# Turning a sixth pair of second-layer weights in the plain part of a retention and two-layer feed-forward kernel

## The chip, the cores and the metric

The kernel runs on one core of one Trainium2 chip. The metric is device time in microseconds (us) of that core; 831.47 us is the median of three runs before the change (830.78 to 833.61). In what follows PE is the matrix engine, PEld its weight loads, DVE the vector engine, ACT the scalar engine, POOL the GpSimd engine and SP the engine that issues most transfers.

## The reference

Retention over 4 batches, 8 heads, 576 positions and a head width of 64, then two feed-forward layers over the 2304 tokens, each 512 to 2048 to 512, all in fp32:

```python
scores = scale * np.matmul(q, k.transpose(0, 1, 3, 2))
ret = scores * Dmat[None, :, :, :]          # decay gamma**(i-j), causal
attn_out = np.matmul(ret, v)
...
h = x @ w_in;  g = np.maximum(h, 0.0) + alpha * np.minimum(h, 0.0);  x = g @ w_out     # layer 1
h = x @ w_in;  g = h * (1.0 / (1.0 + np.exp(-1.702 * h)));           x = g @ w_out     # layer 2
```

## The kernel before

**Stages.** The retention of 16 head pairs runs first, as loop iterations 0 to 16. Then comes the *plain part*: layer 1 on 1536 of the 2304 tokens, in three chunks of 512 tokens, 48 steps. A step is one hidden block of 128 rows: 12 products of `mm1` (h from x and `wi`) and 12 of `mm2` (acc from g and `wo`), the second two steps later. Chunk 0 and 1 use the blocks in pieces (`BLOCKS`); hidden blocks 0 and 1 are used in steps 0 to 3 and then not before step 32, when chunk 2 begins. Then come four *rounds* of 768 tokens. Round 0 is the rest of layer 1, rounds 1 to 3 are layer 2. A round is a two by two block product with seven products in place of eight (Strassen's scheme with sums of blocks), 112 units of 6 products each: units 0 to 55 make the hidden layer (`unit1`), units 56 to 111 the output (`unit2`). Every operand of a product is split into two rounded parts, `hi` and `lo`: ACT copies, DVE subtracts.

**Turning weights.** The weights come as raw 8-byte words, 16 rows of 128 x 1024 for each layer. A row is loaded in two halves of 0.5 MB (`w_piece`), gets three passes on ACT (`w_sat`, `w_range`, `w_top`: L129, L133, L137) and one on DVE (`w_low`, L144). Two rows make a *pair*, and `pair2` plans a pair of layer 2: eight sums of quarters (`p_sums`, L174), a store of the plain quarters to DRAM (`r_store`, tensor `rg`), the `hi` copies on ACT (`b_hi`) and `lo` subtractions on DVE (`b_lo`, L192), and a store of the finished blocks (`b_store`, tensors `sm` and `sp`). Rounds 1 to 3 read these back: `r_load` and `r_split` for the first product of a round, `s_load` (tiles `ws`) for the second. In round 0 the second product reads the layer 1 blocks that `p_store` and `plain_store` wrote.

**What sets the order.** Every engine runs its own program in order. The order is written by hand: `at(time, fn, ...)` puts a piece of work at a time, counted in iterations, in half steps of the plain part (`half(n)`) or in units of the rounds, and `run_to` emits what is due. Loads of `pair2` are issued by POOL's queue in the plain part and by SP's in the rounds; a transfer that must wait for its tile holds up what stands behind it in the same queue. Tiles share places by tag: `w0` holds the first-layer weights `wi[0]` of hidden blocks 0 and 1, `w8` their second-layer weights `wo[0]`, and `cv`, `raw1`, `w1`, `X1` to `X4` take rows in turn.

**Before**, pairs 0 to 4 of layer 2 are turned in the plain part, pair 5 straddles its end and the first half of round 0, pair 6 is turned in round 0 (units 43 to 113) and pair 7 in round 1 (units 117 to 156). In round 0, POOL makes the 16 differences of hidden blocks that the second product needs (`g_sum`), and the two of each hidden pair that `after1` calls `t1` and `t2`. In iteration 4 of the retention ACT's program has the first pass over row 0 of the layer 1 weights (`layer1`, m = 0).

Of the kernel before, what the change touches and what calls it, by code (L numbers as in the profile page):

```python
# [46 lines left out]
def kernel(  # L47
# [11 lines left out]
    nc = tc.nc  # L59
# [28 lines left out]
    r1 = [dram.tile([128, 2, 4, 256], F32, name=f"r1_{j}") for j in range(NJ)]  # L88
    sp = [[dram.tile([128, 3, 4, 2, 256], F32, name=f"sp{n}_{h}") for h in range(2)] for n in (1, 2)]
# [149 lines left out]

    def row(key, src, home, load, when, eng):  # L240
        at(load[0], w_load, key, src, home)
        for c, t in enumerate(load):
            at(t, w_piece, key, src, c, eng)
        for t, fn in zip(when, (w_sat, w_range, w_top, w_low)):
            at(t, fn, key)

    def pair2(j, t, homes, load, rows, sums, store, hi, lo, late, eng):
        for e in range(2):
            row((2, 2 * j + e), w2, homes[e], [t(n) for n in load[e]] if type(load[e]) is tuple else (t(load[e]),) * 2, [t(n) for n in rows[e]], eng)
        for g in range(2):  # L250
            at(t(sums[g]), p_sums, 2, j, g, nc.gpsimd if j > 3 else nc.vector)
        at(t(store), r_store, j)
        for n in range(2):
            at(t(hi[n]), b_hi, j, n)
            at(t(lo[n]), b_lo, j, n)
        at(t(late), b_store, j)
# [381 lines left out]
    def s_load(r, n):  # L638
        i, h = divmod(n, 2)
        t = ws["s", n] = slot(RING[n % (5 if r else 3)], [128, 4, 2, 256], F32R, "ws2")  # L640
        l = min(r, 1)
        src = sm[l][h][:, SUM[i]] if i in SUM else sp[l][h][:, i // 3]
        nc.sync.dma_start(out=t.bitcast(F32), in_=src)
# [172 lines left out]
    for m, home, load, when, hi, lo in (  # L816
        (0, "cv", (2.8, 3.8), (4.75, 5.75, 6.75, 8.0), 8.25, 9.0),
# [40 lines left out]
    for j, n in enumerate((12, 20, 26, 28, 48, 50, 53, 60)):  # L858
        at(half(n), plain_store, j)
    for j, plan in enumerate((  # L860
# [16 lines left out]
    with tc.manual_schedule():  # L877
# [74 lines left out]
        for k in range(NK):  # L952
            at(base + (26.0, 26.4, 29.9, 30.4)[k], x_load, 2, k)
            at(base + (29.7, 30.1, 30.8, 31.2)[k], x_split, 2, k, xp[1])
        for c, home, t in ((1, "X3", 27), (0, "X1", 32)):
            at(base + t, part_load, c, home)
        for k in range(2):
# [5 lines left out]
            5, lambda u: 1e3 + u, ("raw1", "X2"), (3.7, 9),  # L963
            ((22.1, 22.2, 24.1, 25.3), (29.1, 29.2, 31.1, 32.3)), (33, 33.1), 38.6, (43.1, 43.2), (44.3, 45.4), 46.5,
            nc.sync,
        )
# [21 lines left out]
        for j, homes, *plan in (  # L988
# [4 lines left out]
        ):  # L993
            pair2(j, float, homes, *plan, nc.sync)
        for r in range(R):
# [34 lines left out]
            for j in range(8):  # L1030
                at(z + 7.3 + 2.4 * j, g_sum, 0, 4, 0, j, None if r else nc.gpsimd)
                at(z + 25.6 + 2.4 * j, g_sum, 3, 3, 4, j, None if r else nc.gpsimd)
# [82 lines left out]
```

## Time and profile before

| | before |
|---|---|
| median of three runs | 831.47 us |
| the profiled execution: its time, its span | 831.47 us, 829.8 us |
| PE busy | 806.6 us (97%) |
| PEld busy | 745.2 us (90%) |
| DVE busy | 649.4 us (78%) |
| ACT busy | 531.1 us (64%) |
| POOL busy | 124.6 us (15%) |
| moved by DMA | 210.67 MB, 254 GB/s |
| mean granted PE clock | 0.991 |

The span runs from the first to the last instruction; the run's time has 1.7 us more around it. A busy engine is one with an instruction in work; the profile counts products as pipelined, so PE's share says little, and its gaps and the length of a stage say more.

### The profile page before, as it was taken

What the parts mean: (1) busy time and instruction counts of PE and PEld (TensorE: products, weight loads), DVE (VectorE), ACT (ScalarE), POOL (GpSimd) and SP (SyncE); (2) the same over time, 40 slices, a digit from 0 to 9 for tenths busy, and PEclk for the clock granted to TensorE, in tenths of its full rate; (3) what the DMA queues carried; (4) which work ended last, traced back from release to release, by engine and by line L of the source; (5) the groups of instructions that cost most, each with busy time, mean ns of one, the idle gap of its engine ahead of it and who ended that gap; (6) DMA issues with size and microseconds to landing.
All of it is one profiled execution on the core that took longest, in us unless ns stands there. A gap on an engine that the chain in (4) does not pass through costs nothing.

```text
span 829.8 us, 14143 instructions
## 1 busy us (share of the span) xinstructions
PE 806.6 (97%) x5004; PEld 745.2 (90%) x5004; DVE 649.4 (78%) x1157; ACT 531.1 (64%) x961; POOL 124.6 (15%) x134
## 2 busy tenths in 40 slices
PE   9899999999999999899998989999999999999998
PEld 8798888888888888789797989999999999999998
DVE  7587987886475677768999868989777799777875
ACT  7579969775354865454774677766566667566653
POOL 2231111100002106326647003000000000000000
PEclk9999999999999999999998999999999999999999
DMA  9896999635878673986977684988443986445881
GB/s 348 352 359 225 347 368 365 247 147 216 316 245 305 215 264 103 321 312 223 355 276 257 228 270 135 362 316 313 137 134 99 363 308 215 148 130 197 293 270 72
DMA packets 87053, 210.67 MB, mean 254 GB/s; under 512 B 7875, under 2 KB 43715, under 8 KB 78534
## 3 DMA queue, kind: packets, MB, share of 16 engines
q1 hardware_dynamic: 81072, 188.78, 64.1%
q0 software_dynamic: 5760, 20.97, 7.4%
q8 instruction: 39, 0.64, 0.3%
q14 instruction: 32, 0.26, 0.1%
q10 hardware_dynamic: 150, 0.02, 0.0%
HBM read 150.50 MB, written 59.24 MB: 253 GB/s over the span
## 4 chain that ended last, share of the span: by engine, by line
PE 77%; DMA 6%; DVE 5%; issue 3%; ACT 2%; POOL 2%; SPq 1%; POOLq 0%; ACTq 0%; DVEq 0%
PE acc L654 24%; PE h L654 18%; PE h L479 15%; PE acc L520 14%; PE av L318 3%; DMA rg<-raw 1%; POOL raw L174 1%; DMA ws<-r 1%; PE sc L318 1%; PE st L318 1%; DMA raw<-in_w_dram 1%; DVE tm L174 1%; DMA x<-os 1%; DMA ws<-sp 1%; DVE gsf L104 1%
## 5 line engine op out<-in xcount | busy, mean ns | idle before, releaser
L104 DVE TENSOR_TENSOR gsf<-g,gsf 128x384 fp32r<-128x384 f32 (+1 forms) x272 | 169.8, 638 | 39.2 <-ACT gsf L99 38.3
L99 ACT ACTIVATE gsf<-g 128x384 fp32r<-128x384 f32 (+1 forms) x272 | 145.6, 542 | 76.5 <-PE acc L654 32.4
L654 PE MATMUL acc<-gsf,ws 128*128 128x384 f32 x768 | 136.5, 335 | 2.4 <-DVE gsf L104 1.5
L479 PE MATMUL h<-x,wi 128*128 128x512 f32 x576 | 138.2, 389 | 0.0
L520 PE MATMUL acc<-gsf,wo 128*128 128x512 f32 x576 | 138.2, 389 | 0.0
L654 PEld LDWEIGHTS acc<-gsf,ws 128*128 128x128 f32 x768 | 133.3, 188 | 4.2 <-DVE gsf L104 2.9
L654 PE MATMUL acc<-x,ws 128*128 128x384 f32 x660 | 129.9, 337 | 4.1 <-ACT tm L99 4.1
L520 PEld LDWEIGHTS acc<-gsf,wo 128*128 128x128 f32 x576 | 108.0, 188 | 22.8 <-ACT raw L99 0.4
L479 PEld LDWEIGHTS h<-x,wi 128*128 128x128 f32 x576 | 108.0, 188 | 22.5
L654 PEld LDWEIGHTS acc<-x,ws 128*128 128x128 f32 x660 | 116.1, 189 | 6.0 <-ACT tm L99 6.0
L654 PE MATMUL h<-x,ws 128*128 128x384 f32 x540 | 109.1, 337 | 3.8 <-DVE g L487 1.9
L654 PE MATMUL h<-gsf,ws 128*128 128x384 f32 x576 | 106.6, 341 | 3.4 <-DVE gsf L104 3.4
L654 PEld LDWEIGHTS h<-gsf,ws 128*128 128x128 f32 x576 | 101.8, 192 | 6.2 <-DVE gsf L104 6.2
L654 PEld LDWEIGHTS h<-x,ws 128*128 128x128 f32 x540 | 95.4, 189 | 4.7 <-issue 2.2
L487 DVE SCALAR_TENSOR_TENSOR g<-g,rise_sb,h 128x512 f32<-128x512 f32 (+1 forms) x49 | 36.4, 743 | 52.2 <-ACT g L492 52.0
L174 DVE TENSOR_TENSOR tm<-h,tm 128x384 f32<-128x384 f32 x97 | 53.5, 552 | 26.3 <-PE h L654 22.5
L492 ACT ACTIVATE g<-h 128x512 f32<-128x512 f32 (+1 forms) x49 | 29.1, 594 | 54.7 <-PE h L479 54.7
L174 DVE TENSOR_TENSOR g<-g 128x384 f32<-128x384 f32 x96 | 54.0, 563 | 0.7
L99 ACT ACTIVATE tm<-acc 128x384 f32<-128x384 f32 x62 | 30.3, 488 | 37.7 <-PE acc L654 34.2
L125 POOL DMA_DIRECT2D raw<-in_w_dram x40 | 21.1, 533 | 196.4 <-ACT raw L137 44.2
L104 DVE TENSOR_TENSOR ws<-pad,ws 128x512 fp32r<-128x512 f32 x66 | 39.7, 622 | 9.2 <-ACT ws L99 9.2
L174 POOL TENSOR_TENSOR g<-g 128x384 f32<-128x384 f32 x32 | 40.4, 1280 | 40.0 <-DVE g L487 38.5
(101 smaller groups left out, 979.7 us busy)
## 6 DMA issues: line engine op xcount, KB each, us to landing
ws<-sm SPq DMA_DIRECT2D x32, 1024.0 KB, 6.5
ws<-sp SPq DMA_DIRECT2D x24, 1024.0 KB, 5.6
raw<-in_w_dram POOLq DMA_DIRECT2D x40, 512.0 KB, 7.7
sm<-raw SPq DMA_DIRECT2D x32, 512.0 KB, 4.7
raw<-in_w_dram SPq DMA_DIRECT2D x24, 512.0 KB, 7.8
pad<-rg SPq DMA_DIRECT2D x48, 256.0 KB, 2.8
ld<-in_qkv_dram SPq DMA_DIRECT2D x13, 864.0 KB, 7.5
r<-raw SPq DMA_DIRECT2D x16, 512.0 KB, 3.1
```

What stands on the lines that cost most here:

```text
L99: return nc.scalar.activation(out=out, in_=in_, func=ACTF.Copy)
L104: latest[0] = eng.tensor_tensor(out=out, in0=a, in1=b.bitcast(F32), op=ALU.subtract)
L125: eng.dma_start(out=raws[key][:, c * DM:c * DM + DM], in_=f[:, c * DM:c * DM + DM])
L174: latest[0] = (eng or nc.vector).tensor_tensor(out=out, in0=x, in1=y, op=op)
L318: return nc.tensor.matmul(out=out, lhsT=lhsT, rhs=rhs, start=start, stop=stop, skip_group_check=True)
L479: nc.tensor.matmul(out=t, lhsT=w[:, cw, k * 128:k * 128 + 128], rhs=x[:, cx], start=(i == 0), stop=(i == 3 * NK - 1),)
L487: nc.vector.scalar_tensor_tensor(out=g[0], in0=g[1], scalar=rise_sb[:, m:m + 1], in1=h, op0=ALU.mult, op1=ALU.add)
L492: nc.scalar.activation(out=out, in_=in_, func=ACTF.Relu, scale=-1.0)
L520: nc.tensor.matmul(out=acc[0][d], lhsT=w[:, d // 2, cw, d % 2 * 128:d % 2 * 128 + 128], rhs=g[:, cx], start=(m == m0 and i == 0), stop=(m ...
L654: nc.tensor.matmul(out=out, lhsT=w(cw), rhs=x(cx), start=(start and n == 0), stop=True, skip_group_check=True,)
```

## The change

One more pair of layer 2 is turned in the plain part. Places `w0` and `w8` are lent to it: `wi[0]` and half of `wo[0]` are written to DRAM at the end of the retention (`evict`; the rest of `wo[0]` lies there anyway, since `plain_store(0)` moves ahead), pair 0 is turned in their place in steps 14 to 27, and they are read back on POOL's queue in steps 29.5 and 31 (`bring_wi`, `bring_wo`), before step 32 uses them. The old pairs 0 to 4 become 1 to 5, pair 6 takes the straddling plan of the old pair 5, and pair 7 has its loads and ACT passes in the second half of round 0 and the rest in the first half of round 1. `g_sum` of round 0 goes from POOL to DVE, and so do the sums of pair 7; other stores, the x splits of chunk 2 and the place of a partial sum move; the first passes over row 0 of layer 1 move from iterations 4 to 6 of the retention to 6 to 7.

```diff
+    def evict(j):
+        nc.sync.dma_start(out=kept[j // 2][0], in_=wi[j].bitcast(F32))
+        nc.sync.dma_start(out=kept[j // 2][1], in_=wo[j].bitcast(F32)[:, 1, 0])
+
+    def bring_wi(j):
+        wi[j] = wp.tile([128, 2, 2, DM], F32R, tag=f"w{HOME[j]}", name="wi")
+        nc.gpsimd.dma_start(out=wi[j].bitcast(F32), in_=kept[j // 2][0])
+
+    def bring_wo(j):
+        wo[j] = wp.tile([128, 2, 2, 2, 256], F32R, tag=f"w{8 + j}", name="wo")
+        w = wo[j].bitcast(F32)
+        nc.gpsimd.dma_start(out=w[:, 0], in_=sp[0][0][:, 0:2, j])
+        nc.gpsimd.dma_start(out=w[:, 1, 1], in_=sp[0][0][:, 2, j])
+        nc.gpsimd.dma_start(out=w[:, 1, 0], in_=kept[j // 2][1])
...
-            at(t(sums[g]), p_sums, 2, j, g, nc.gpsimd if j > 3 else nc.vector)
+            at(t(sums[g]), p_sums, 2, j, g, nc.gpsimd if j in (5, 6) else nc.vector)
...
-        (0, "cv", (2.8, 3.8), (4.75, 5.75, 6.75, 8.0), 8.25, 9.0),
+        (0, "cv", (2.8, 3.8), (6.25, 6.75, 7.75, 8.0), 8.25, 9.0),
...
-    for j, n in enumerate((12, 20, 26, 28, 48, 50, 53, 60)):
+    for j, n in ((1, 33), (2, 36), (3, 42), (4, 44), (5, 67), (6, 76), (7, 78)):
         at(half(n), plain_store, j)
+    at(14.0, plain_store, 0)
+    at(14.5, evict, 0)
+    for j, n in ((0, 59),):
+        at(half(n), bring_wi, j)
+        at(half(n + 3), bring_wo, j)
     for j, plan in enumerate((
...
+        (("w0", "w8"), (28, 30), ((35, 42, 43, 46), (43, 44, 45, 47)),
+         (48, 50), 51, (53, 53), (54, 54), 55),
...
         pair2(
-            5, lambda u: 1e3 + u, ("raw1", "X2"), (3.7, 9),
+            6, lambda u: 1e3 + u, ("raw1", "X2"), (3.7, 9),
...
+        pair2(
+            7, lambda u: 1e3 + u, ("X4", "raw1"), ((58.2, 62.2), (66.2, 70.2)),
+            ((72, 75, 78, 114), (82, 86, 90, 121)), (128, 135), 137, (143, 150), (144, 151.5), 153, nc.sync,
         )
...
-        for j, homes, *plan in (
-            (6, ("X4", "raw1"), (43.5, (53, 56)), ((58.5, 61, 64, 66), (66.5, 69.5, 72.5, 75)),
-             (75.5, 75.6), 82, (87, 91), (90, 94), 113),
-            (7, ("raw1", "X4"), (117.1, 118), ((127.1, 129.1, 134.2, 137.3), (127.2, 134.1, 136.1, 138.4)),
-             (139, 139.1), 145, (150.1, 152.1), (151.5, 153.5), 156),
-        ):
-            pair2(j, float, homes, *plan, nc.sync)
...
-                at(z + 7.3 + 2.4 * j, g_sum, 0, 4, 0, j, None if r else nc.gpsimd)
-                at(z + 25.6 + 2.4 * j, g_sum, 3, 3, 4, j, None if r else nc.gpsimd)
+                at(z + 7.3 + 2.4 * j, g_sum, 0, 4, 0, j, None)
+                at(z + 25.6 + 2.4 * j, g_sum, 3, 3, 4, j, None)
```

The line numbers of the changed kernel are higher (L99 becomes L103, L104 becomes L108, L125 becomes L129, L129 becomes L133, L174 becomes L178, L643 becomes L662). Three places show how instructions move.

**ACT, iterations 4 to 7 of the retention.** `kts` are keys, scaled for the pair after next, `r` and `x`, `xs` are the outputs of a head pair, `raw` is row 0 of layer 1. First before, then after:

```order
L282 ACTIVATE r<-st,vtab_sb 128x320
L282 ACTIVATE kts<-kts,vtab_sb 128x4x64 x2
L99 ACTIVATE x<-av 128x512
L99 ACTIVATE x<-av 128x64
L129 ACTIVATE raw<-raw 128x1024
L282 ACTIVATE r<-st,vtab_sb 128x320
L282 ACTIVATE kts<-kts,vtab_sb 128x4x64 x2
L99 ACTIVATE x<-av 128x448
```

```order
L103 ACTIVATE x<-av 128x512
L103 ACTIVATE x<-av 128x64
L301 ACTIVATE r<-st,vtab_sb 128x320
L301 ACTIVATE kts<-kts,vtab_sb 128x4x64 x2
L103 ACTIVATE x<-av 128x448
L103 ACTIVATE xs<-av 128x128
L301 ACTIVATE r<-st,vtab_sb 128x320
L301 ACTIVATE kts<-kts,vtab_sb 128x4x64 x2
L133 ACTIVATE raw<-raw 128x1024
```

The first pass over `raw` now stands behind the keys of two more head pairs.

**DVE, the second half of round 0.** `gsf` are the split hidden blocks that PE reads, `g_3242` and its like the hidden blocks (other numbers after the change), `raw` a row of a layer 2 pair, `x` and `pad` the blocks of x for the next round. First before, then after:

```order
L104 TENSOR_TENSOR gsf<-g_3524,gsf 128x384
L144 SCALAR_TENSOR_TENSOR raw<-raw 128x1024
L104 TENSOR_TENSOR gsf<-g_3604,gsf 128x384
L104 TENSOR_TENSOR x_3036<-pad,x_3036 128x384
L104 TENSOR_TENSOR gsf<-g_3679,gsf 128x384
L174 TENSOR_TENSOR pad<-pad 128x384
```

```order
L178 TENSOR_TENSOR g_3288<-g_3288 128x384
L108 TENSOR_TENSOR gsf<-g_3498,gsf 128x384
L108 TENSOR_TENSOR gsf<-g_3570,gsf 128x384
L178 TENSOR_TENSOR g_3359<-g_3359 128x384
L108 TENSOR_TENSOR gsf<-g_3650,gsf 128x384
L108 TENSOR_TENSOR x_3082<-pad,x_3082 128x384
L108 TENSOR_TENSOR gsf<-g_3722,gsf 128x384
L178 TENSOR_TENSOR pad<-pad 128x384
```

The pass over a raw row is gone from here, and the `g_sum` differences have come from POOL.

**SP, from the end of the first half of round 0.** `ws` from `sp` or `sm` is an `s_load` of 1 MB, `pad` a load of x, `raw` half a row of a pair. First before, then after:

```order
L643 DMA ws_3722<-sp_0_111 128x2048
L643 DMA ws_3724<-sp_1_112 128x2048
L125 DMA raw<-in_w_dram 128x1024 x2
L643 DMA ws_3803<-sm_0_115 128x2048
```

```order
L662 DMA ws_3843<-sm_0_117 128x2048
L600 DMA pad<-x_0_89 128x512
...
L129 DMA raw<-in_w_dram 128x1024
L662 DMA ws_3888<-sm_1_118 128x2048
L129 DMA raw<-in_w_dram 128x1024
L662 DMA ws_3928<-sm_0_117 128x2048
L129 DMA raw<-in_w_dram 128x1024
L662 DMA ws_3970<-sm_1_118 128x2048
L129 DMA raw<-in_w_dram 128x1024
```

The four halves of the pair now stand one by one between the weight loads of the running product.

## Rows read from the trace of the kernel before

**Rows 1.** Busy time by stage: length, each engine's busy time, PE clock, DMA share, GB/s.
```profile
0.00:72.25 72.25, 67.78 (x1165) 60.20 (x1165) 53.49 (x125) 50.41 (x106) 19.02 (x22) 0.98 0.92 345
72.25:333.79 261.54, 261.54 (x1157) 216.24 (x1153) 190.19 (x296) 174.99 (x241) 36.46 (x54) 1.00 0.72 257
333.79:400.52 66.73, 60.16 (x338) 57.91 (x336) 51.88 (x84) 33.18 (x65) 26.14 (x25) 1.00 0.85 294
400.52:469.85 69.33, 64.45 (x336) 60.17 (x337) 66.43 (x96) 43.80 (x87) 35.20 (x26) 0.95 0.77 274
469.85:534.87 65.02, 61.29 (x338) 59.64 (x337) 51.40 (x93) 48.13 (x91) 7.82 (x8) 0.97 0.72 247
534.87:593.11 58.24, 58.24 (x338) 58.24 (x337) 52.22 (x108) 38.51 (x80) 0.00 (x0) 1.00 0.79 279
593.11:651.35 58.24, 58.24 (x338) 58.24 (x337) 44.40 (x87) 36.36 (x77) 0.00 (x0) 1.00 0.49 158
```

**Rows 2.** Timeline of PE in the retention: start, length, instructions, wait ahead.
```profile
23.97 1.16 PE L318 MATMUL sc<-ld 64*128 64x128 f32 x16
...
27.70 1.16 PE L318 MATMUL sc<-ld 64*128 64x128 f32 x16
32.01 1.02 PE L318 MATMUL st<-ld,kts 128*64 128x64 f32 x15 [3.15 <-ACT kts L282]
...
36.47 1.29 PE L318 MATMUL sc<-ld 64*128 64x128 f32 x16
```

**Rows 3.** Timeline of ACT there.
```profile
30.01 1.14 ACT L129 ACTIVATE raw<-raw 128x1024 f32<-128x1024 f32 x1 [4.84 <-DMA raw<-in_w_dram]
```

**Rows 4.** DVE's groups by form, 400 to 470 us: count, busy us, mean ns.
```profile
L104 DVE TENSOR_TENSOR gsf<-g,gsf 128x384 fp32r<-128x384 f32 x54 | 41.9, 808 | 1.4 <-ACT gsf L99 1.4
```

**Rows 5.** Timeline of POOL in the second half of round 0.
```profile
403.26 10.20 POOL L174 TENSOR_TENSOR g<-g 128x384 f32<-128x384 f32 x8 [4.69 <-DVE g L487]
...
437.11 13.50 POOL L174 TENSOR_TENSOR g<-g 128x384 f32<-128x384 f32 x10
```

**Rows 6.** Timeline of PE at the start of that half.
```profile
400.52 4.78 PE L654 MATMUL acc<-gsf,ws 128*128 128x384 f32 x26 [0.97 <-DMA ws<-sp]
406.21 4.82 PE L654 MATMUL acc<-gsf,ws 128*128 128x384 f32 x22 [0.92 <-DVE gsf L104]
```

**Rows 7.** ACT's groups, 469.85 to 534.87 us.
```profile
L681 ACT ACT_TABLE_LOAD x2 | 2.6, 1283 | 0.0
...
L129 ACT ACT_TABLE_LOAD x1 | 1.3, 1283 | 0.0
```

**Rows 8.** Timeline of PE in the first half of round 1.
```profile
492.94 1.31 PE L654 MATMUL acc<-x,ws 128*128 128x384 f32 x6 [2.12 <-ACT tm L99]
494.09 2.05 PE L654 MATMUL h<-x,ws 128*128 128x384 f32 x6
```

**Rows 9.** DVE's groups by form, 534 to 592 us (second half of round 1).
```profile
L104 DVE TENSOR_TENSOR gsf<-g,gsf 128x384 fp32r<-128x384 f32 x55 | 29.5, 553 | 3.4 <-ACT gsf L99 3.2
L174 DVE TENSOR_TENSOR g<-g 128x384 f32<-128x384 f32 x18 | 9.9, 551 | 0.0
```

**Rows 10.** Groups by form in the plain part.
```profile
L174 DVE TENSOR_TENSOR raw<-raw 128x256 f32<-128x256 f32 x88 | 33.3, 420 | 0.8
L144 DVE SCALAR_TENSOR_TENSOR raw<-raw 128x1024 int32<-128x1024 int32 x24 | 29.2, 1218 | 2.2 <-ACT raw L137 2.2
...
L129 ACT ACTIVATE raw<-raw 128x1024 f32<-128x1024 f32 x22 | 25.2, 1144 | 0.0
```

**Rows 11.** Busy time in two stretches of the plain part, columns as in the first group.
```profile
160.00:200.00 40.00, 40.00 (x178) 33.14 (x177) 31.14 (x51) 24.89 (x35) 1.05 (x2) 1.00 0.51 187
200.00:240.00 40.00, 40.00 (x178) 33.10 (x178) 21.93 (x34) 20.80 (x28) 3.04 (x6) 1.00 0.72 251
```

**Rows 12.** Transfers by kind: count, KB of one, median us from issue to landing.
```profile
ws<-sm SPq DMA_DIRECT2D x32, 1024.0 KB, 6.5
...
raw<-in_w_dram SPq DMA_DIRECT2D x24, 512.0 KB, 7.8
```

**Rows 13.** Busy time at the start of the second half of round 0, columns as in the first group.
```profile
400.00:408.00 8.00, 6.57 (x35) 5.99 (x36) 7.81 (x11) 6.57 (x12) 4.66 (x4) 1.00 1.01 378
```

More of the change, by code (lines that the diff above doesn't have):

```diff
@@ L88 @@
     r1 = [dram.tile([128, 2, 4, 256], F32, name=f"r1_{j}") for j in range(NJ)]
+    kept = [
+        (dram.tile([128, 2, 2, DM], F32, name=f"ki_{j}"), dram.tile([128, 2, 256], F32, name=f"ko_{j}"))
+        for j in range(1)
+    ]
     sp = [[dram.tile([128, 3, 4, 2, 256], F32, name=f"sp{n}_{h}") for h in range(2)] for n in (1, 2)]
@@ L639, in s_load @@
         i, h = divmod(n, 2)
-        t = ws["s", n] = slot(RING[n % (5 if r else 3)], [128, 4, 2, 256], F32R, "ws2")
+        t = ws["s", n] = slot(RING[n % 5] if r else RING[n % 3], [128, 4, 2, 256], F32R, "ws2")
         l = min(r, 1)
@@ L952 @@
         for k in range(NK):
-            at(base + (26.0, 26.4, 29.9, 30.4)[k], x_load, 2, k)
-            at(base + (29.7, 30.1, 30.8, 31.2)[k], x_split, 2, k, xp[1])
-        for c, home, t in ((1, "X3", 27), (0, "X1", 32)):
+            at(base + (25.0, 25.2, 27.8, 28.2)[k], x_load, 2, k)
+            at(base + (27.3, 27.7, 29.1, 29.5)[k], x_split, 2, k, xp[1])
+        for c, home, t in ((1, "raw1", 26.8), (0, "X1", 32)):
             at(base + t, part_load, c, home)
@@ L962 @@
         pair2(
-            5, lambda u: 1e3 + u, ("raw1", "X2"), (3.7, 9),
+            6, lambda u: 1e3 + u, ("raw1", "X2"), (3.7, 9),
             ((22.1, 22.2, 24.1, 25.3), (29.1, 29.2, 31.1, 32.3)), (33, 33.1), 38.6, (43.1, 43.2), (44.3, 45.4), 46.5,
             nc.sync,
+        )
+        pair2(
+            7, lambda u: 1e3 + u, ("X4", "raw1"), ((58.2, 62.2), (66.2, 70.2)),
+            ((72, 75, 78, 114), (82, 86, 90, 121)), (128, 135), 137, (143, 150), (144, 151.5), 153, nc.sync,
         )
```

14 rows, old and new, of the table step_us are left out of this document.

## The prediction

> **What bounds the kernel now.** I read the busy times by stage first [rows 1]. The reader is to see that PE is the clock of the whole kernel: in the plain part it is busy for all of 261.54 us, and the two half rounds from 534.87 us on take 58.24 us each with no gap. A half round has 56 units of 6 products of 384 columns, so 58.24 us is what PE needs for one. The three half rounds before have the same products and take 66.73, 69.33 and 65.02 us: they lose 8.49, 11.09 and 6.78 us, 26.4 together. Outside them only the retention can lose much. So the change can only win in four places, and I ask in each what makes PE wait.
>
> In the retention a head pair takes 3.73 us (27.70 less 23.97) until iteration 6, where the next scores come 8.77 us later, so 5.04 us are lost once [rows 2]. PE waits 3.15 us for keys that ACT scales, and then runs some products at the lower clock. ACT is late because its program has the first pass over row 0 of layer 1 ahead of them, and that pass waited 4.84 us for its load [rows 3].
>
> In the second half of round 0 DVE is busy for 66.43 of 69.33 us [rows 1]. Its subtraction for `gsf` takes 808 ns there and 553 in the same half of round 1 [rows 4, 9]. What differs is POOL, which works on `g` for 10.20 us from 403.26 and 13.50 from 437.11 [rows 5] and not at all in round 1 [rows 1]. So DVE's demand is the same and its speed beside POOL is not.
>
> In the first half of round 1 PE waits 2.12 us at 492.94 for ACT, and then a unit of six products takes 2.05 us in place of 1.31 [rows 8]. ACT there has three table loads of 1.28 us [rows 7]: one into the table of layer 2's activation, and two around the first passes over pair 7.
>
> **The change part by part.**
>
> *Retention.* The first pass over row 0 moves to iteration 6, behind the keys of two more pairs. The load landed at about 30.0 (the pass began at 30.01) [rows 3]; the new place in the program is reached some 3 us after the scores at 27.70 [rows 2], about 30.5. No wait is left, so the 5.04 us go. Lower bound of the gain: transfers. The stage moves 345 GB/s over 72.25 us [rows 1], 24.9 MB, and `plain_store(0)` (0.8 MB) and `evict` (1.3 MB) are added at its end. At 378 GB/s, the fastest stretch I show [rows 13], 27.0 MB take 71.5 us, which would leave a gain of 0.8. I take 5.0, since the added stores stand behind the last query load on SP, and the retention reads nothing after that; what they can delay are rows 4 and 5 of layer 1, whose passes come in steps 0 to 2.
>
> *Plain part.* Added for pair 0: on ACT six passes of 1.14 us and `hi` copies of about 2, 9 us; on DVE two passes of 1.22, eight sums of 0.42 and `lo` subtractions of about 2.4, 8.2 us [rows 10]. They fall into steps 17 to 27, about 162 to 216 us. There DVE is idle for 8.9 of 40 and 18.1 of 40 us, ACT for 15.1 and 19.2 [rows 11]. The sums of the old pair 4's place in the plan, 3.4 us, also come to DVE later. PE does not wait as long as an activation is done within a step and a half, so I cost all this at nothing; without that cover it would be up to 9 us. The later pairs shift by one and keep their old times almost to the half step. `x_load` and `x_split` of chunk 2 move 2 to 3 steps ahead of use. The load of x for k = 3 now stands on SP behind four stores of a partial sum, and ACT's split of step 29 stands behind that x; I allow 3 us of waiting on ACT there, less than the step of 5.45 us (261.54 / 48) that `mm2` comes later.
>
> `bring_wi` is a new wait for PE. Step 32 begins 62 blocks of 12 products into the part: 72.25 + 62 x 2.724 = 241.1 us. Pair 0's last `lo` is due at step 27, 52 blocks in: 213.9. A store and a 1 MB load behind it, 7.8 us each at worst by the medians [rows 12], end at 229.5. That leaves 11.6 us; cost nothing. Behind `bring_wi` on POOL stand the loads of pairs 2 to 5, due from step 30 on.
>
> *First half of round 0.* Pair 6 takes the plan of pair 5 with the same times, POOL's sums, `t1` and `t2` included. The half-rows of the old pair 6 that were loaded in units 43 to 56 are gone. I leave the loss of 8.49 us as it is, with 2 us either way.
>
> *Second half of round 0.* Gone: two DVE passes and the `lo` of the old pair 6, and all of POOL but the two differences of the last hidden pair. Added on DVE: 16 differences at 0.55 us, 8.8 us alone, less back to back [rows 9]. The row to go by is the same half of round 1: with all 16 differences on DVE and the same x blocks, DVE is busy 52.22 of 58.24 us, and PE loses nothing [rows 1]. ACT has 38.51 us there and gets six passes, 6.9: 45.4 of 58.24. What stays are the waits at its start: 0.97 us for the first `ws`, behind pair 6's stores as before, and 0.92 for `gsf`, where the rest of the first half still runs into it [rows 6]. With the first product after a wait I count 2.3 us for these two. Gain 11.09 - 2.3 = 8.8; bounds 0 (DVE stays the limit) and 11.1.
>
> *First half of round 1.* Gone: two table loads, six ACT passes, 9.4 us of ACT in all [rows 7, 10]; POOL's sums; and the wait of SP on the old pair 6's late store. Added on DVE: eight sums, 3.4 us, beside the passes and `lo` that were there. The same half of round 2 has DVE at 44.40 of 58.24 us without loss [rows 1], 13.8 idle; pair 7 takes two passes 2.4, sums 3.4, `lo` 2.4, 8.2 in all, in six bursts about 7 units apart. They fit; each burst may hold up an activation a little, so I keep 1.0 us (bounds 0 and 8.2). Gain 6.78 - 1.0 = 5.8.
>
> **Sum**, against the profiled execution, whose 831.47 us is also the median of the runs: 831.47 - 5.0 - 8.8 - 5.8 = 811.9 us.
>
> **The rivals.**
>
> *Weights late in round 0's second half.* Four half-rows of 0.52 MB are now issued between `s_load`s that are needed 8 units after their issue. At 378 GB/s [rows 13] each takes 1.4 us, and what they delay adds up: at most 5.5 us, 817.4 us. For it: the stretch already moves 378 GB/s at a DMA share of 1.01. Against: at that speed a 1 MB load takes 2.8 us of the 4.2 that four units last, so 1.4 us remain per load, which is just one half-row. 12 in 100. The Trainium skill's page DMA: Bandwidth & Descriptors, section Specifications, gives about 358 GB/s as a core's share of the memory. By that rule, as an estimate, a load and a half-row would take 4.4 us of the 4.2, so this rival would come true in part, with about 1 us over four units, 813. The measured 378 is above the rule, and the measurement decides.
>
> *Retention bound by its transfers.* The gain there is the 0.8 us of the lower bound: 816.1 us. For it: a DMA share of 0.92 [rows 1]. Against: the place of the added stores. 12 in 100.
>
> *The change does not free DVE or ACT.* If DVE with 16 more differences stays the limit in round 0, 8.8 us are not won: 820.7. If it is the bursts in round 1, 817.7. 6 in 100. The idle times of rounds 1 and 2 speak against both.
>
> *Slower.* `wi[0]` comes back so late that PE stands at step 32. POOL's queue is in order: were `bring_wi` held behind a raw load whose place is not free, nothing else would bring the weights. It decides when the landing is 11.6 + 19.6 = 31 us later than I reckon, 261 us in place of 229.5; at 40 us late the time would be 811.9 + 28 = 840. For it: a chain of store, queue and load that no run has shown. Against: the loads ahead of it belong to places that come free by step 26 as before. 4 in 100.
>
> The forecast gets 62 in 100, and 4 are left for better, if the first half of round 0 loses less as well.
>
> **How the numbers follow.** The time is the forecast's, 812. The range 806 to 822 holds the forecast with the bounds of its small terms, the first three rivals, and the better case down to 2 us in the first half of round 0 and the last waits; it leaves out the slower case and mishaps that join. A difference of under 0.3% (2.5 us) can't be told from no change here. Faster: all cases but the slower one, less 2 for several losses together, 94 in 100; same 2; slower 4.
>
> **What the profile after would show.** Retention 67.2 us long, with scores 3.73 us apart in iteration 6 and no wait on the first pass. Plain part 261.5, PE without a gap at step 32. First half of round 0 about 66.7; second half 60.5, with POOL silent after its first differences and `gsf` near 553 ns; first half of round 1 59.2, with one table load. The forecast is wrong if PE waits on `ws` in round 0 (first rival), if the query loads land just ahead of their scores (second), if DVE stays over 95% busy in round 0's second half (third), or if a wait of PE on `wi` or an ACT wait on a raw load stands in the plain part.

## The result and the profile after

| | before | after |
|---|---|---|
| median (four runs each, side by side) | 832.4 us | 811.52 us (811.16 to 812.25) |
| ratio, 95% interval | | 0.9751 (0.973 to 0.9772) |
| the profiled execution: time, span | 831.47, 829.8 us | 811.16, 809.5 us |
| DVE, ACT, POOL busy | 649.4, 531.1, 124.6 us | 644.2, 526.8, 88.2 us |
| moved by DMA | 210.67 MB, 254 GB/s | 214.08 MB, 264 GB/s |

The kernel is 20.9 us faster by the medians and 20.3 by the profiled spans. The forecast was 812.0. The busy times by stage after the change, with the columns of [rows 1]:

```profile
0.00:66.97 66.97, 65.58 (x1164) 58.34 (x1165) 53.75 (x125) 50.01 (x106) 19.07 (x22) 1.00 0.99 385
66.97:329.86 262.89, 261.82 (x1157) 216.20 (x1153) 196.85 (x309) 180.74 (x250) 40.32 (x62) 1.00 0.80 284
329.86:395.48 65.62, 61.24 (x338) 59.63 (x337) 50.93 (x82) 33.23 (x64) 26.44 (x25) 0.97 0.80 277
395.48:456.15 60.67, 59.10 (x337) 58.14 (x337) 54.41 (x110) 42.64 (x84) 2.38 (x2) 1.00 0.89 322
456.15:514.39 58.24, 58.24 (x337) 58.24 (x337) 52.02 (x101) 39.89 (x83) 0.00 (x0) 1.00 0.65 211
```

Against [rows 1] the retention is 5.28 us shorter, the plain part 1.35 longer, the two halves of round 0 are 1.11 and 8.66 shorter and the first half of round 1 is 6.77 shorter, 20.47 in all (the end of the kernel takes 0.17 longer). That last stage now has the bare 58.24 us of its products: nothing is lost there any more.

In the retention the scores now come 3.73 us apart through the place where 8.77 stood [rows 2]. PE's timeline, other rows left out:

```profile
27.59 1.16 PE L337 MATMUL sc<-ld 64*128 64x128 f32 x16
...
31.32 1.16 PE L337 MATMUL sc<-ld 64*128 64x128 f32 x16
...
35.05 1.16 PE L337 MATMUL sc<-ld 64*128 64x128 f32 x16
```

ACT's timeline has the first pass over row 0 two pairs of keys later, with no wait ahead of it; before it waited 4.84 us [rows 3]:

```profile
31.11 0.90 ACT L301 ACTIVATE kts<-kts,vtab_sb 128x256 f32<-128x256 f32 x2
31.91 1.17 ACT L133 ACTIVATE raw<-raw 128x1024 f32<-128x1024 f32 x1
```

In the second half of round 0 DVE's groups by form are those of [rows 9]; before, the first of them took 808 ns [rows 4]:

```profile
L108 DVE TENSOR_TENSOR gsf<-g,gsf 128x384 fp32r<-128x384 f32 x55 | 29.9, 566 | 2.4 <-ACT gsf L103 2.2
L178 DVE TENSOR_TENSOR g<-g 128x384 f32<-128x384 f32 x16 | 8.8, 552 | 0.0
```

POOL has only `t1` and `t2` of the last hidden pair left there, in place of [rows 5]:

```profile
399.34 2.46 POOL L178 TENSOR_TENSOR g<-g 128x384 f32<-128x384 f32 x2 [4.69 <-PE acc L673]
```

PE's timeline of that half round shows two waits at the start, 0.19 and 1.23 us, both for `gsf`, and from there on no gap. The wait for the first `ws` [rows 6] is gone:

```profile
395.48 2.59 PE L673 MATMUL acc<-gsf,ws 128*128 128x384 f32 x14
398.26 2.78 PE L673 MATMUL acc<-gsf,ws 128*128 128x384 f32 x12 [0.19 <-DVE gsf L108]
402.27 4.11 PE L673 MATMUL acc<-gsf,ws 128*128 128x384 f32 x22 [1.23 <-DVE gsf L108]
406.22 8.48 PE L673 MATMUL h<-gsf,ws 128*128 128x384 f32 x48
```

The one new wait of PE is in the plain part, 1.07 us at 222.6:

```profile
219.72 2.88 PE L498 MATMUL h<-x,wi 128*128 128x512 f32 x12
223.67 2.99 PE L539 MATMUL acc<-gsf,wo 128*128 128x512 f32 x12 [1.07 <-ACT gsf L103]
```

ACT's timeline tells why. At 206.9 us it comes to pair 0's `hi` copies and waits 5.52 us for the store of the plain quarters that they overwrite. Then it is behind, and the three passes over pair 1's second row (219.39 to 223.16) run ahead of the copy that PE wants:

```profile
206.32 0.60 ACT L511 ACTIVATE g<-h 128x512 f32<-128x512 f32 x1 [1.06 <-PE h L498]
212.44 1.89 ACT L103 ACTIVATE raw<-raw 128x1024 fp32r<-128x1024 f32 x3 [5.52 <-DMA rg<-raw]
...
219.39 1.13 ACT L133 ACTIVATE raw<-raw 128x1024 f32<-128x1024 f32 x1
220.56 1.11 ACT L137 ACTIVATE raw<-raw 128x1024 f32<-128x1024 f32 x1
221.56 0.58 ACT L511 ACTIVATE g<-h 128x512 f32<-128x512 f32 x1
222.04 1.12 ACT L141 ACTIVATE raw<-raw 128x1024 int32<-128x1024 uint8 x1
223.04 0.62 ACT L103 ACTIVATE gsf<-g 128x512 fp32r<-128x512 f32 x1
```

`wi` was issued at 221.7 and landed 5.4 us later, at 227.1. The first products that use it begin at 237.38 us, so 10 us were left; the prediction had 11.6.

### The profile page after: what moved, and what is told of

It is laid out like the page before. It is cut to its first block, busy times and chain, and to the rows that moved or that the text cites. A ratio compares the mean times of both kernels' runs of the same rounds, so it can differ in the third digit from the quotient of the medians.

```text
span 809.5 us, 14137 instructions
## 1 busy us (share of the span) xinstructions
PE 797.3 (99%) x5004; PEld 741.6 (92%) x5004; DVE 644.2 (80%) x1189; ACT 526.8 (65%) x959; POOL 88.2 (11%) x110
## 2 busy tenths in 40 slices
DMA packets 87789, 214.08 MB, mean 264 GB/s; under 512 B 7971, under 2 KB 43811, under 8 KB 79014
## 4 chain that ended last, share of the span: by engine, by line
PE 85%; DMA 5%; DVE 4%; ACT 2%; issue 1%; SPq 1%; POOL 1%; ACTq 0%; DVEq 0%; POOLq 0%
PE acc L673 28%; PE h L673 22%; PE h L498 14%; PE acc L539 13%; PE av L337 4%; DMA ws<-r 2%; PE sc L337 2%; PE st L337 2%; DMA sp<-raw 1%; DVE g L506 1%; DMA rg<-raw 1%; DVE raw L196 1%; DVE tm L178 1%; DMA ld<-in_qkv_dram 1%; DVE gsf L108 1%
## 5 line engine op out<-in xcount | busy, mean ns | idle before, releaser
L108 DVE TENSOR_TENSOR gsf<-g,gsf 128x384 fp32r<-128x384 f32 (+1 forms) x272 | 157.5, 591 | 51.3 <-ACT gsf L103 50.0
L103 ACT ACTIVATE gsf<-g 128x384 fp32r<-128x384 f32 (+1 forms) x272 | 145.9, 541 | 78.1 <-PE acc L673 32.8
L673 PE MATMUL h<-gsf,ws 128*128 128x384 f32 x576 | 101.8, 334 | 0.0
L673 PEld LDWEIGHTS h<-gsf,ws 128*128 128x128 f32 x576 | 100.0, 188 | 0.0
L178 DVE TENSOR_TENSOR tm<-h,tm 128x384 f32<-128x384 f32 x97 | 53.7, 554 | 26.5 <-PE h L673 22.3
L178 DVE TENSOR_TENSOR g<-g 128x384 f32<-128x384 f32 x112 | 62.0, 554 | 0.7
L103 ACT ACTIVATE tm<-acc 128x384 f32<-128x384 f32 x62 | 30.4, 490 | 41.0 <-PE acc L673 37.2
L178 DVE TENSOR_TENSOR raw<-raw 128x256 f32<-128x256 f32 x112 | 42.4, 420 | 1.0
L129 POOL DMA_DIRECT2D raw<-in_w_dram x44 | 23.2, 533 | 174.0 <-DVE raw L178 52.9
L148 DVE SCALAR_TENSOR_TENSOR raw<-raw 128x1024 int32<-128x1024 int32 x32 | 39.0, 1218 | 2.2 <-ACT raw L141 2.2
```

What stands on the lines that cost most here:

```text
L103: return nc.scalar.activation(out=out, in_=in_, func=ACTF.Copy)
L108: latest[0] = eng.tensor_tensor(out=out, in0=a, in1=b.bitcast(F32), op=ALU.subtract)
L129: eng.dma_start(out=raws[key][:, c * DM:c * DM + DM], in_=f[:, c * DM:c * DM + DM])
L148: latest[0] = nc.vector.scalar_tensor_tensor(out=g[:, 0:2 * DM], in0=t[:, :, 1], scalar=3, in1=t[:, :, 0], op0=ALU.logical_shift_left, op1 ...
L178: latest[0] = (eng or nc.vector).tensor_tensor(out=out, in0=x, in1=y, op=op)
L673: nc.tensor.matmul(out=out, lhsT=w(cw), rhs=x(cx), start=(start and n == 0), stop=True, skip_group_check=True,)
```

## The experiments

Stage lengths of each profiled execution, in us (bold: where the edit aims or acts):

| run | retention | plain part | round 0, first | round 0, second | round 1, first | time | ratio to before |
|---|---|---|---|---|---|---|---|
| before | 72.25 | 261.54 | 66.73 | 69.33 | 65.01 | 831.47 | |
| after | 66.97 | 262.89 | 65.62 | 60.67 | 58.24 | 811.16 | 0.9751 (0.973 to 0.9772) |
| retention alone | **68.90** | 261.53 | 67.09 | 68.97 | 66.17 | 829.27 | 0.9958 (0.9943 to 0.9974) |
| differences on DVE | 72.08 | 261.53 | 68.79 | **67.18** | 64.88 | 831.09 | 0.997 (0.9954 to 0.9986) |
| differences on POOL | 67.77 | 263.02 | 65.95 | **64.35** | 58.24 | 816.11 | 0.982 (0.9801 to 0.9839) |
| passes in round 1 | 67.10 | 262.96 | 65.79 | 60.73 | **66.08** | 819.43 | 0.9878 (0.9857 to 0.9898) |
| no table | 68.69 | 263.02 | 66.19 | 61.11 | **61.13** | 816.93 | 0.9824 (0.9795 to 0.9853) |
| back behind load | 67.20 | **271.37** | 67.77 | 60.94 | 58.24 | 822.29 | one run |
| rows twice | 68.39 | 263.23 | 65.49 | **78.84** | 58.24 | 830.68 | 0.9968 (0.9956 to 0.9979) |
| more traffic | 67.14 | 263.17 | 67.35 | **65.18** | 58.24 | 817.58 | 0.9817 (0.9788 to 0.9846) |
| three waits | 67.64 | **268.13** | **67.42** | **58.53** | 58.24 | 816.73 | 0.9817 (0.979 to 0.9845) |
| POOL silent | 66.97 | **267.36** | **69.83** | **58.89** | 58.24 | 818.09 | 0.9833 (0.9807 to 0.986) |
| other three | 67.60 | **262.04** | **70.21** | **60.35** | 58.24 | 814.97 | 0.9781 (0.9763 to 0.9799) |
| two edits | 67.04 | **262.61** | **68.03** | **60.77** | 58.24 | 813.47 | 0.9791 (0.9767 to 0.9816) |

Stages that no edit touches tell how far one execution can be trusted: the retention of the changed kernel spreads from 66.97 to 68.69, its first half of round 0 from 65.49 to 67.77, the other stages by 0.5.

### The retention alone

```diff
-        (0, "cv", (2.8, 3.8), (4.75, 5.75, 6.75, 8.0), 8.25, 9.0),
+        (0, "cv", (2.8, 3.8), (6.25, 6.75, 7.75, 8.0), 8.25, 9.0),
```

> The kernel before with one edit of the change: the first pass over row 0 in iteration 6 of the retention. My theory: the lost time there is ACT's wait on that load, so the scores of iteration 6 come 3.73 us after the ones before, the retention takes 67 us in place of 72.25, and the whole gains 5.0 to 5.3 us (ratio 0.994). The rival: the stage is held by its transfers, which then take the place of that wait; it gains at most 0.8 us.

3.5 us came by the ratio of the runs (0.9958; the medians, 827.8 and 832.17, are 4.4 apart), 3.35 by the stage. The wait is gone: PE's timeline has the scores 3.73 us apart through iteration 6. What is missing is at the start, where one iteration's scores took 2.08 us and not 1.16:

```profile
10.54 2.08 PE L318 MATMUL sc<-ld 64*128 64x128 f32 x16
14.43 1.16 PE L318 MATMUL sc<-ld 64*128 64x128 f32 x16
...
25.78 1.16 PE L318 MATMUL sc<-ld 64*128 64x128 f32 x16
29.51 1.16 PE L318 MATMUL sc<-ld 64*128 64x128 f32 x16
```

From the scores at 14.43 to the end of the stage at 68.90 are 54.5 us. In the changed kernel it is 12.48 to 66.97, 54.5 as well, and before 12.58 to 72.25, 59.7. So the edit is worth 5.2 us, the start varies from run to run, and the stores that the change adds at the end cost nothing, although the stage now moves 385 GB/s: the rival of the transfers falls.

### Round 0: the differences on DVE or on POOL

The kernel before with this edit, and the changed kernel with the edit turned round:

```diff
-                at(z + 7.3 + 2.4 * j, g_sum, 0, 4, 0, j, None if r else nc.gpsimd)
+                at(z + 7.3 + 2.4 * j, g_sum, 0, 4, 0, j, None)
```

(and the same in the line below it.)

> The kernel before with one edit of the change: the 16 differences of hidden blocks that round 0's second product needs are made on DVE and not on POOL; pair 6 stays in that half round, with its sums on POOL. My theory: DVE is the limit there because its operations take longer while POOL works, so the mean of the gsf subtraction falls from 808 to below 650 ns and the half round from 69.33 to 62 to 65 us (4 to 7 us won). The rival: DVE is the limit by the number of its operations, and 16 more (8.8 us) beside pair 6's two passes and subtractions make the half round longer, 70 to 75 us.

> The changed kernel with these 16 differences back on POOL, all else as changed. My theory: POOL's 16 operations of 1.2 us again stretch DVE's beside them; the gsf mean in that half round goes from below 600 to about 700 ns, and the half round from 60.67 to 62 to 66 us. The rival: moving pair 6's passes out of the half round was all that was needed, and DVE has room for the stretch; the half round stays within 1 us of 60.67.

The second stood as expected: `gsf` went back to 772 ns and the half round to 64.35 us.

```profile
L108 DVE TENSOR_TENSOR gsf<-g,gsf 128x384 fp32r<-128x384 f32 x55 | 40.5, 772 | 2.3 <-ACT gsf L103 2.3
```

The first gave 2.15 us of the 4 to 7. Its DVE did what was expected; all of the half round's 54 `gsf` subtractions:

```profile
L104 DVE TENSOR_TENSOR gsf<-g,gsf 128x384 fp32r<-128x384 f32 x54 | 29.4, 566 | 8.9 <-ACT gsf L99 8.7
```

But the loss came back in another place. Pair 6's eight sums, still on POOL there, took 17.23 us in POOL's timeline (before, 11.76; the last section says why):

```profile
425.53 17.23 POOL L174 TENSOR_TENSOR raw<-raw 128x256 f32<-128x256 f32 x8 [18.08 <-DVE raw L144]
```

Pair 6's store, and the `hi` copies that overwrite what it reads, came late. ACT's timeline, and PE's behind it:

```profile
443.02 1.06 ACT L99 ACTIVATE raw<-raw 128x1024 fp32r<-128x1024 f32 x1 [7.75 <-DMA rg<-raw]
```

```profile
444.54 7.08 PE L654 MATMUL h<-gsf,ws 128*128 128x384 f32 x30 [4.45 <-ACT gsf L99]
```

The four corners are 69.33 (both on POOL), 67.18 (differences moved), 64.35 (pair 6 moved) and 60.67 (both moved). Either move alone wins 2.15 or 4.98, both together 8.66. The third corner is the changed kernel with the differences turned back, so pair 6's two DVE passes and subtractions are gone there together with its sums on POOL; no run moved the sums alone. With the differences alone left on POOL the stage takes 3.7 us more than with both moved, and with pair 6 alone left in it 6.5.

### Round 1: passes, tables, sums

The changed kernel, with pair 7's times in round 1 those of before; then the same with two further edits.

```diff
-            ((72, 75, 78, 114), (82, 86, 90, 121)), (128, 135), 137, (143, 150), (144, 151.5), 153, nc.sync,
+            ((127.1, 129.1, 134.2, 137.3), (127.2, 134.1, 136.1, 138.4)),
+            (139, 139.1), 145, (150.1, 152.1), (151.5, 153.5), 156, nc.sync,
```

> The changed kernel with pair 7's loads where the change puts them (second half of round 0), but with its six ACT passes, its sums, splits and store at the times they had before, in round 1; the sums stay on DVE. My theory: the 6.77 us that the first half of round 1 lost are ACT's: two table loads of 1.28 us and passes in a burst ahead of the copies that PE waits for; 3.5 to 5.5 us of them come back, most around units 18 to 25 of the half round, where PE waits for tm. The rival: they were late loads and POOL's sums, both of which stay away here; the half round stays within 1 us of 58.24.

7.84 us came back, more than the 3.5 to 5.5 expected, in two places. Around units 18 to 26 of the half round it is 3.5 us, and ACT's timeline shows the burst: a table load, two passes, and only then the copy `tm` for PE, which waited 1.74 us for it; a second load follows.

```profile
473.35 1.28 ACT L133 ACT_TABLE_LOAD   x1
474.64 2.15 ACT L133 ACTIVATE raw<-raw 128x1024 f32<-128x1024 f32 x2
476.69 1.13 ACT L103 ACTIVATE ws<-pad 128x512 fp32r<-128x512 f32 x2
477.73 0.47 ACT L103 ACTIVATE tm<-acc 128x384 f32<-128x384 f32 x1
478.10 1.15 ACT L137 ACTIVATE raw<-raw 128x1024 f32<-128x1024 f32 x1
479.26 1.28 ACT L700 ACT_TABLE_LOAD   x1
```

Around units 32 to 34 it is 4.3 us, which I had not expected: all eight sums stand together on DVE, ahead of what PE needs next.

```profile
490.96 3.01 DVE L178 TENSOR_TENSOR raw<-raw 128x256 f32<-128x256 f32 x8
```

```diff
+        if key[0] == 2 and key[1] > 13:
+            nc.scalar.activation(out=f, in_=f, func=ACTF.Copy, scale=2.0 ** -9)
+            return
...
-            (139, 139.1), 145, (150.1, 152.1), (151.5, 153.5), 156, nc.sync,
+            (139, 146), 148, (150.1, 152.1), (151.5, 153.5), 156, nc.sync,
```

> The run that puts pair 7's ACT passes into round 1, with two edits. The first passes of pair 7 are plain scaled copies of the same size (they don't limit the values, so that part of the function is left out) and need no other table; and the two groups of four sums stand seven units apart and not together. The run with the passes lost 3.5 us around units 18 to 26 of the half round and 4.3 around units 32 to 34. If the two table loads are the cause of the first, it falls below 1 us; if the passes alone are, it stays above 2. If the burst of eight sums is the cause of the second, it falls below 1 us; if any sum or subtraction there costs, it stays above 2. Half round: 59 us by the first of each, 65 by the second.

The half round took 61.13 us. At the first place 1.18 us of 3.50 stayed, so taking out the two table loads, 2 x 1.28 us, gave back 2.3. At the second 1.34 of 4.34 stayed, so some 70% of it was the burst. Both rests lie just above the 1 us that I had set: the table loads and the burst are the main part of each loss, and the lone passes and sums cost the rest. The Trainium skill (ScalarE: Activation LUTs, What ACT_TABLE_LOAD costs) adds a drain of some 1.38 us to each load; the rows show the next pass 0.01 us after the load's end, and 2.3 us for two loads are no more than their 1.28 each.

These runs give sizes, but they are not the whole loss of the kernel before. There PE stood 0.75 us at 482.5, ahead of any pass over pair 7, because ACT was waiting for a load:

```profile
481.56 1.26 ACT L99 ACTIVATE ws<-pad 128x512 fp32r<-128x512 f32 x2 [2.28 <-DMA pad<-rg]
```

By PE's timeline of that kernel, 4.5 of the 6.78 us went between 490 and 503 us, where the table loads and the passes stand; 1.0 went behind this load, 0.6 at 515, right behind POOL's sums, and 0.5 at 525, behind the `hi` copies. So by these places the rival, late loads and POOL's sums, may have had some 1.6 us of it; no run took these away alone.

### The return of the weights

```diff
-    for j, n in ((0, 59),):
+    for j, n in ((0, 63),):
```

> The changed kernel with the return of wi and wo two steps later in POOL's program, behind the raw load of pair 2's first row, which can't start before about 231.9 us. This is the mechanism that the prediction priced as its slower case. By my reckoning wi is issued at about 233 us and lands at 239 to 241, PE needs it at 237.1, so PE stands 2 to 4 us at step 32; wo lands ahead of its need at 250.7 and costs nothing. The rival: there is more room than reckoned, and the plain part stays at 262.9 us.

The mechanism came true and cost more: PE waited 5.73 us, and the 12 products behind the wait took 5.18 us in place of 2.88, with a granted clock of 0.55 in 244 to 249 us. The plain part grew by 8.5 us, in the one execution that there is of this kernel.

```profile
243.79 5.18 PE L498 MATMUL h<-x,wi 128*128 128x512 f32 x12 [5.73 <-DMA wi<-ki]
```

`wi` was issued at 231.4, earlier than I reckoned, but took 12.4 us to land behind the two raw loads in its queue, not the 5.4 of the changed kernel. (Of `wo[0]` the detour through `ko` takes a quarter, `w[:, 1, 0]`, and not half, as the description of the change has it; the 1.3 MB of `evict` are right.)

### Is there room for the half-rows?

First each half-row of pair 7 was loaded twice; then each load got a copy from DRAM to DRAM behind it, for which nothing waits.

```diff
+        for _ in range(2 if key[0] == 2 and key[1] > 13 else 1):
...
+        if key[0] == 2 and key[1] > 13:
+            extra = dram.tile([128, DM, 2], I32, name=f"ex_{key[1]}_{c}")
+            eng.dma_start(out=extra, in_=f[:, c * DM:c * DM + DM])
```

> The changed kernel with every half-row of pair 7 loaded twice, 2 MB more in the second half of round 0, on the same queue and between the same weight loads. My theory: the transfers there have room, so the half round grows by less than 1 us from 60.67. The rival (weights late): each half-row more holds up the weights behind it by 1.4 us, the delays add up, PE waits for ws, and the half round grows by 3 to 5.5 us.

18.2 us, far above both. It is not transfers: the second load writes where the first does, so SP's queue stands between them, about 7 us each time, and the weights stand behind.

```profile
399.87 8.11 SPq L130 DMA_DIRECT2D raw<-in_w_dram  x2
408.08 0.38 SPq L663 DMA_DIRECT2D ws<-sm  x1
408.51 7.28 SPq L130 DMA_DIRECT2D raw<-in_w_dram  x2
415.88 0.38 SPq L663 DMA_DIRECT2D ws<-sm  x1
```

> The changed kernel with a copy of each half-row of pair 7 from DRAM to another place in DRAM behind its load, four of 0.5 MB on the same queue; no later work reads them, and nothing on the queue waits for them. In the run that loaded the half-rows twice, the second load waited on SP for the first (both write one place) and held up the weights behind it, so it did not measure transfers alone. In the changed kernel's trace the weight loads of units 68 to 88 land 0.6 to 1.3 us ahead of their use. If that is all the room there is, each copy makes the loads behind it 1.4 us or more later, PE waits for ws around units 68 to 84, and the half round grows by 3 to 6 us from 60.67. If the loads only land late because the queue has no reason to hurry, it grows by less than 1 us.

The half round grew by 4.5 us, with a wait of 2.75 for `ws`:

```profile
423.78 4.40 PE L676 MATMUL acc<-gsf,ws 128*128 128x384 f32 x24 [2.75 <-DMA ws<-sm]
```

So the half-rows fit once and not with the same again behind them; a copy also writes its 0.5 MB to DRAM, so it is a harder test than a second half-row. The rival "weights late" fell by about a microsecond of room for each load.

### Can the last waits be taken away?

Three edits for the three waits of PE that are left, and the same with all of POOL's arithmetic from the end of the plain part on DVE:

```diff
-         (48, 50), 51, (53, 53), (54, 54), 55),
+         (48, 50), 51, (55, 55), (56, 56), 57),
...
-            6, lambda u: 1e3 + u, ("raw1", "X2"), (3.7, 9),
+            6, lambda u: 1e3 + u, ("raw1", "X2"), (7.2, 9),
...
-            add(gblk(1, j), gblk(1, j), gblk(0, j), ALU.subtract, None if r else nc.gpsimd)
+            add(gblk(1, j), gblk(1, j), gblk(0, j), ALU.subtract)
```

(`t2` likewise; with POOL silent also `eng = None` in `x2_step` and `nc.vector` for all sums.)

> The changed kernel with three edits, each aimed at one wait of PE that its trace shows, at three places that can be told apart. (a) Pair 0's hi copies, lo subtractions and store stand one step later: my theory is that ACT's 5.52 us wait for pair 0's store at 206.9 us pushes pair 1's passes ahead of a copy that PE needs at 222 us, so the wait of 1.07 us there goes and the plain part falls from 262.89 to 261.6 us; by the rival (the passes are simply too many there) it stays. (b) Pair 6's first row is loaded behind the fourth r1 load and not ahead of it: SP then does not stand until 350.7 us for pair 5's store, and PE's 1.84 us at unit 21 go; by the rival (the transfers are slow there) most of it stays. (c) t1 and t2 of round 0 are made on DVE: the 1.5 us at unit 60 fall below 0.5. All three: 4 us below the changed kernel, 807.5 us; by the rivals within 1 us of it.

> The run with the three edits, and POOL's other arithmetic from the end of the plain part on DVE too: the differences of x for round 0 and the sums of pairs 5 and 6. My theory: what POOL does costs DVE about as much time as doing it itself, and the chain of x differences that releases the first r1 load gets shorter, so the 2.14 us at unit 0 fall by 1 us or more, and the kernel is 1 to 3 us faster than with the three edits alone. The rival: DVE, with 12 sums of 0.42 us and 8 differences of 0.55 us more, delays the copies of the last steps and of the first units, and the kernel is 1 us or more slower than with the three edits.

(a) took the wait at 222 us away, which confirms its cause, and put a larger one at step 32 (3.90 us with POOL silent, which has the same edit):

```profile
240.37 5.49 PE L498 MATMUL h<-x,wi 128*128 128x512 f32 x12 [3.50 <-DMA wi<-ki]
```

One step (5.4 us) of delay for pair 0's store became 13.2 us for `wi`, which was issued at 232.6 and landed at 240.3: the store now stood on SP behind four stores of a partial sum, and store and load each took longer to land. (b) took the wait at unit 21 away, but PE then ran into others: 0.8 us more at unit 32, where ACT's passes over pair 6's second row stand ahead of `tm`, and 0.90 for the first `ws` of the second half. (c) took the second half to 58.53 us, 0.28 above the bare products, but PE now lost 1.5 us at units 44 to 46 of the first half, where it lost nothing in the changed kernel: the two halves together took 125.95 us, before these edits 126.29. Silencing POOL shortened unit 0's loss from 1.96 to 1.12 us, lost 1.3 at unit 7 for the next of these loads, and lost 3.13 us at unit 37, where all eight sums of pair 6 stand together on DVE for 3.01 us, as pair 7's did in round 1: the rival, by one burst.

```diff
-        (("cv", "w1"), (46, 53), ((51, 51, 52, 53), (56, 56, 57, 58)),
+        (("cv", "w1"), (46, 53), ((51, 51, 52, 53), (58, 58, 58, 59)),
...
-            nc.sync,
+            nc.gpsimd,
```

> The changed kernel with three edits at the same three places as in the run with three waits, two of them other ones. (a) Pair 0 stays as changed; the passes over the second row of pair 1 stand one step later, behind the copy that PE waited for at 222 us: if that burst is the cause, the plain part falls from 262.89 to 261.6 us and the return of wi is no later; if ACT's wait for pair 0's store is the whole cause, the wait of PE stays. (b) Pair 6's loads are issued by POOL and not by SP, so that the r1 loads do not stand behind them and the rows come no later: the 1.84 us at unit 21 go without the new waits that the later loads brought. (c) t1 and t2 of round 0 on DVE, which took the second half of round 0 to 58.5 us. Together 807 us, 4 to 5 below the changed kernel; if the rows from POOL collide as the later ones did, 809 to 811.

(a) worked in its new form (262.04 us): a later store of pair 0 or later passes of pair 1, either takes the wait at 222 us away, so it takes both to make it. (b) collided again: ACT waited 3.34 us for the first row, and PE lost 2.94 behind it. (c) lost the same 1.5 us at units 44 to 46, and the second half took 60.35 us, not 58.5.

> The changed kernel with the two edits that worked at their place in the runs before: the passes over pair 1's second row one step later, and t1 and t2 of round 0 on DVE; pair 6's loads stay where the change has them. I expect the plain part at 261.6 to 262.0 us, the second half of round 0 at 58.5 to 59.5, the rest as in the changed kernel: 808 to 809.5 us, faster than both kernels. By the rival, DVE's 16 more operations in the first half of round 0 take back there what is won later, and it is within 1 us of 811.5.

The rival. 813.47 us; the interval overlaps that of the changed kernel, and the profile says why nothing was won. The wait at 222 us is gone, and 0.6 us were lost at 233. At the start of the second half 1.0 us was lost in place of 2.4, and 1.3 us of losses for `ws` came at units 95 and 99; in the first half, with DVE busy for 56.06 us in place of 50.93, units 44 to 46 lost 1.5, as in the two runs before with this edit and POOL's other work in place. So (c) alone does not give 58.5 us: that came with the other edits of the two runs that have it, and the two without them stand at 60.35 and 60.77. No version tried beats the changed kernel.

## Why the prediction was right, and where it was off

- **Retention**: 5.0 forecast, 5.28 measured, and 5.2 by the experiment, once the start is left out. Right, and for the reason given. The 378 GB/s of the lower bound were no bound: the stage now moves 385 on average.
- **Plain part**: "I cost all this at nothing" was mis-sized, 1.35 us. The sum of busy times left room; what I missed is ACT's 5.52 us of waiting for pair 0's own store, which pushes the next pair's passes together. (One other pair has such a wait in this trace, 0.84 us.) In all seven kernels with the changed order at this place PE loses 1.2 to 1.6 us there. I had allowed 3 us of waiting on ACT at another place, the split of x for step 29: it waited 7.39 us there, at 232.06, more than the step of 5.45, and PE still lost nothing; with two edits it lost 0.6 behind that wait. That term came out by luck.
- **The return of `wi`**: 10 us of room where 11.6 were forecast, so nothing was lost. The price of the slower case (each microsecond late costs one) was too low: 5.73 us of waiting cost 8.5, since the products after the wait run at a granted clock near half.
- **First half of round 0**: "I leave the loss of 8.49 us as it is" was 1.1 off, within the 2 us allowed and within the 2.3 by which this stage varies. One difference is not chance: the last unit lost 1.13 us waiting for the first `ws`, 1.48 and 1.33 in the two kernels built on the one before, and nothing in the changed kernel and the six that keep its plan here. I had kept the wait for the first `ws` because pair 6's stores stand ahead of it as before. What I had noted but not counted is that the half-rows of the old pair 6 behind it are gone: the first load for the half now landed 5.6 us after its issue, before 7.0, and in both kernels was wanted 6.0 after it (395.48 less 389.41, and 399.39 less 393.35). That these half-rows caused it is read from the traces; no run tried it alone.
- **Second half of round 0**: 8.8 forecast, 8.66 measured. The four corners show the mechanism (DVE is stretched by POOL's work) and that it takes both moves. The 2.3 us left for the start came out in size by luck: 0.97 for `ws` and 0.92 for `gsf` were forecast, and measured are nothing for `ws` and 1.42 for `gsf`, 2.4 lost with the products behind them. The rival "the change does not free DVE" fell: DVE is busy 54.41 of 60.67 us there.
- **First half of round 1**: 5.8 forecast, 6.77 measured; the 1.0 us kept for bursts was nothing. The experiments give sizes: table loads 2.3 us, the other passes 1.2, and sums in a burst would have cost 3 more. That the change has them in two groups of four is what made the burst term zero. The rest of what the kernel before lost there, a late load and POOL's sums among it, went too, as listed under "Gone", and is not tested part by part.
- **Weights late**: the rival fell, but by little. "1.4 us remain per load, which is just one half-row" was borne out: with a copy of 0.5 MB more for each half-row the half round costs 4.5 us, near the 5.5 of its price.

## What to carry to other kernels

An engine's share of busy time doesn't say what a burst costs: in the changed kernel four sums and four cost nothing, where eight in one place came with a loss of 4.3 us, and lone passes cost nothing, where passes with two table loads lost 3.5. Work taken off a shared resource pays when all of it goes: 16 of POOL's 26 operations gave a quarter of the gain, because what stayed came later. And where the remaining waits are about 1 us and the loads behind them land 1 us early, taking one wait away moves PE into the next: ask what has the next smallest margin before an edit, and expect nothing if it is of the same size.

## What the runs showed of the hardware

POOL and DVE took turns, once POOL had come in. Before, in 437.1 to 450.6 us, POOL's ten differences took 1.35 us each, and DVE's subtractions beside them 1324 ns where they take 550 alone.

```profile
L104 DVE TENSOR_TENSOR gsf<-g,gsf 128x384 fp32r<-128x384 f32 x8 | 10.2, 1324 | 0.0
```

Here POOL came in when DVE paused. In the same kernel, a little earlier, the first of pair 6's sums stood for 4.68 us while DVE ran back to back at 550 ns. DVE then stood still for 0.13 us (429.46 to 429.59); the sum ended 0.5 us later, and from there each of DVE's operations took 1.09 us and each sum about 1.0:

```profile
425.38 4.68 POOL L174 TENSOR_TENSOR raw<-raw 128x256 f32<-128x256 f32 x1 [11.92 <-ACT gsf L99]
```

```profile
428.91 0.55 DVE L104 TENSOR_TENSOR gsf<-g,gsf 128x384 fp32r<-128x384 f32 x1
429.59 0.89 DVE L104 TENSOR_TENSOR x<-pad,x 128x384 fp32r<-128x384 f32 x1
430.40 1.09 DVE L104 TENSOR_TENSOR gsf<-g,gsf 128x384 fp32r<-128x384 f32 x1
```

The run with the retention alone shows the same 4.68 us, ended by a pause of 0.12. With the differences on DVE, DVE had no pause until 437.11: one sum on POOL stood for 12.19 us, while DVE ran its operations back to back at 550 ns and was not slowed at all; then DVE waited for ACT, and POOL's other seven took 0.72 us each (17.23 less 12.19, by seven).

```profile
425.53 12.19 POOL L174 TENSOR_TENSOR raw<-raw 128x256 f32<-128x256 f32 x1 [18.08 <-DVE raw L144]
```

```profile
L104 DVE TENSOR_TENSOR gsf<-g,gsf 128x384 fp32r<-128x384 f32 x13 | 6.8, 550 | 0.0
```

The Trainium skill (SBUF — State Buffer, Who interferes with whom) has it that a DVE operation with two inputs in SBUF contends with a GpSimd operation that reads SBUF, that the ports they share are an exclusive lock, and that the order of issue decides who is blocked. The taking of turns agrees with that. The 12.19 us are more than one instruction: some 24 of DVE's went by. In these three traces DVE's first pause ended the wait; no run was built to test it, and the profile's times on POOL are rough.

A late load can cost more than its wait: after PE's 3.50 us for `wi` in the run with three waits the granted clock was 0.50 in 240.4 to 246 us, the lower of its two levels (1.2 of 2.4 GHz), and 12 products took 5.49 us, not 2.88. It does not always: after the 2.75 us for `ws` in the run with more traffic the clock was 1.00 in 423.8 to 428 us.
